# Transposes of queries, keys and attention values moved from TensorE to the DMA crossbar in a fused attention and token-mixing kernel

## The chip, the cores and the metric

One core of one Trainium2 chip. The metric is the device time of one execution in microseconds (us). Runs of one kernel agree within about 1.5%. Each ratio to the kernel before is taken on the same chip. Some times below are compared across chips; the kernel before had medians of 261.9 to 262.5 us.

## The reference

Grouped-query attention (8 batches, 16 query heads, 4 key/value heads, 384 tokens, head size 64), then a token-mixing layer on its output x (384 x 1024 per batch):

```python
scores = scale * q @ k.T;  attn = softmax(scores);  x = attn @ v       # per head; k, v shared by 4 heads
wq, wk = x @ w_q, x @ w_k                                              # 1024 -> 64
mixed = (scale * wq @ wk.T) @ x
out = relu(mixed) @ w_out                                              # 1024 x 1024
```

## The kernel before

All eight batches run through one software pipeline. A "duo" is two key/value heads with their eight query heads; a batch has two duos, each 3 x 3 score steps. Two steps make a **group**; a batch has nine, numbered 0 to 8 here. In each group TensorE issues the scores of two steps, ScalarE their exponentials, then TensorE does the tasks planned for that group and fills the rest of a budget with pieces of the previous batch's output projection ("filler", 48 matmuls per batch).

Three kinds of operand have to be transposed, and all are transposed on TensorE against an identity and copied out of PSUM by VectorE:

```python
def qt_task(s, d, j):                                   # queries; kt_task (keys) is alike
    ptr = psX.tile([P, G, P], BF16, name="ptq", tag="ps")
    for i in range(G):
        nc.tensor.transpose(out=ptr[:, i, :], in_=s.qbf[:, d, j, i, :, :].rearrange("p h d -> p (h d)"),
                            identity=ident)
    # ... (qT allocated)
    nc.vector.tensor_copy(out=s.qT[d][:, j, :, :], in_=ptr)

def xt_task(s, d, j):                                   # attention values, before the projection
    # ... four transposes of xnat into ptx
    nc.vector.tensor_copy(out=s.xT[:, n * d:n * (d + 1), j * P:(j + 1) * P], in_=ptr)

# planning: what runs in which group, with its cost in us
def start_next():                                       # in group 0 of batch b
    alloc_bf(batches[b + 1]); begin(batches[b + 1])
    if b + 2 < B: batches.append(load(b + 2))           # eight DMAs on SyncE's queue, 2.4 MB
# ...
at(g, lambda ...: av_task(batches[b], d, j, h), 0.37)   # attention x values
at(g + 1, lambda ...: xt_task(batches[b], d, j), 0.24)
# ...
at(g, lambda ...: kt_task(batches[nb], nd), 0.18)
at(g + j, lambda ...: qt_task(batches[nb], nd, j), 0.24)

SLOT = 2.0                                              # budget of a group
def fill(budget, keep=0):                               # pieces of output projection
    while filler and budget > 0 and left[0] > keep:
        next(filler[0]); budget -= 0.218; left[0] -= 1
# ... per batch: projection (proj) in group 2 of the next batch, wk in 3, c in 4,
#     mixing + ReLU in groups 5 and 6, then its output projection becomes the filler
```

A range test on the softmax sums chooses, at the end, whether a slow general path must run. It never does with this input.

## Time and profile before

| | before |
|---|---|
| time, median of 4 runs | 262.5 us |
| TensorE busy | 88% of the span |
| ScalarE, VectorE, GpSimd busy | 64%, 54%, 18% |
| one batch in the steady state | 29.6 us |
| mean granted TensorE clock | 0.98 |

The groups of instructions of the profile page show what the change removes. Columns: line, engine, operation, out<-in, shapes, count | busy us, mean ns of one | idle time before, and who ended it.

```profile
L181 DVE COPY xT<-ptx 128x512 bf16<-128x512 bf16 x48 | 20.4, 424 | 33.9 <-PE ptx L179 33.9
L141 DVE COPY qT<-ptq 128x512 bf16<-128x512 bf16 x48 | 19.9, 415 | 3.2 <-PE ptq L136 3.2
L179 PE MATMUL ptx<-ident,xnat 128*128 128x128 bf16 x192 | 19.3, 222 | 0.9 <-DVE xnat L170 0.9
L136 PE MATMUL ptq<-ident,qbf 128*128 128x128 bf16 x192 | 19.2, 224 | 0.5 <-DVE qbf L103 0.5
```

So 38.5 us of TensorE's busy time and 40.3 us of VectorE's go to these two kinds alone.

### The profile page before, as it was taken

How to read it: one execution, taken by the hardware profiler on the slowest of the kernel's cores; microseconds unless marked ns; L12 is line 12 of the kernel's file. 1: busy time of each engine (PE TensorE's matmuls, PEld its weight loads, DVE VectorE, ACT ScalarE, POOL GpSimd, SP SyncE). 2: the span in 40 equal slices, each digit the busy share in tenths (PEclk: the TensorE clock that was granted, in tenths of full speed). 3: DMA queues.
4: the chain of work that ended last, by engine and by line, in shares of the span. 5: the costliest groups of instructions: out<-in, count | busy, mean ns of one | idle time of the engine just before them, and what ended most of it. 6: DMA issues, size and time to landing. Idle time of an engine off the chain costs nothing.

```text
span 261.7 us, 5872 instructions
## 1 busy us (share of the span) xinstructions
PE 230.6 (88%) x2423; PEld 118.5 (45%) x2457; DVE 141.5 (54%) x388; ACT 166.9 (64%) x186; POOL 46.9 (18%) x105
## 2 busy tenths in 40 slices
PE   2988887999889997999889997999889998959892
PEld 1455543455435543455435543455445553433340
DVE  2367663566546664566546664566556563453531
ACT  2889897677757687577766687577766687500201
POOL 1797133052003220052002220040000000000000
PEclk9999999999999999999999999999999999977998
DMA  7999998293107801293107902101012202101224
GB/s 200 326 299 241 228 267 252 98 313 116 65 18 241 281 4 80 81 316 132 47 36 227 293 3 83 80 8 78 31 52 83 83 0 83 80 0 67 96 101 149
DMA packets 33712, 34.26 MB, mean 131 GB/s; under 512 B 4624, under 2 KB 29712, under 8 KB 33680
## 3 DMA queue, kind: packets, MB, share of 16 engines
q1 hardware_dynamic: 29184, 30.94, 36.5%
q0 software_dynamic: 3168, 2.36, 5.8%
q10 hardware_dynamic: 1328, 0.52, 0.7%
q8 instruction: 21, 0.34, 0.5%
q14 instruction: 11, 0.09, 0.1%
HBM read 23.59 MB, written 12.58 MB: 138 GB/s over the span
## 4 chain that ended last, share of the span: by engine, by line
PE 73%; ACT 14%; DVE 8%; issue 2%; DMA 1%; DVEq 0%; ACTq 0%
PE po L236 30%; PE sc L149 14%; PE av L164 11%; ACT msb L225 8%; ACT pT L155 6%; PE ptx L179 5%; PE pqk L187 5%; DVE xnat L170 3%; PE ptq L136 3%; PE pc L207 2%; DMA qraw<-in_q_dram 1%; PE pm L219 1%; DVE xT L181 1%; DVE rcp_all L169 1%; PE ptw L198 1%
## 5 line engine op out<-in xcount | busy, mean ns | idle before, releaser
L155 ACT ACTIVATE pT<-sc 128x1024 bf16<-128x1024 f32 x144 | 139.1, 1024 | 45.6 <-PE sc L149 44.9
L236 PE MATMUL po<-wout_sb,msb 128*128 128x512 bf16 x350 | 91.0, 385 | 6.6 <-ACT msb L225 4.7
L149 PE MATMUL sc<-qT,kT 64*128 64x512 bf16 x288 | 48.6, 394 | 9.4 <-ACT msb L225 5.0
L236 PEld LDWEIGHTS <-msb 128*128 128x128 bf16 x384 | 34.1, 99 | 46.7 <-ACT msb L225 9.3
L249 DVE COPY osb<-po 128x512 f32<-128x512 f32 x46 | 31.8, 690 | 38.9 <-PE po L236 38.6
L164 PE MATMUL av<-vbf,pT 128*128 128x65 bf16 x1152 | 45.4, 195 | 0.0
L164 PEld LDWEIGHTS <-pT 128*128 128x128 bf16 x1152 | 40.7, 98 | 9.4 <-issue 9.4
L170 DVE TENSOR_TENSOR xnat<-av,rcp_all 128x256 bf16<-128x256 f32 x96 | 40.8, 425 | 3.3
L181 DVE COPY xT<-ptx 128x512 bf16<-128x512 bf16 x48 | 20.4, 424 | 33.9 <-PE ptx L179 33.9
L103 POOL CAST qbf<-qraw 128x512 bf16<-128x512 f32 x46 | 26.9, 622 | 38.9 <-DMA qraw<-in_q_dram 17.4
L225 ACT ACTIVATE msb<-pm 128x768 bf16<-128x768 f32 x30 | 22.8, 809 | 14.2 <-PE pm L219 14.2
L149 PEld LDWEIGHTS <-kT 64*128 64x128 bf16 x288 | 11.5, 94 | 40.0 <-issue 37.0
L169 DVE RECIPROCAL rcp_all<-av 128x4 f32<-128x4 f32 x96 | 17.1, 178 | 17.7 <-PE av L164 17.7
L141 DVE COPY qT<-ptq 128x512 bf16<-128x512 bf16 x48 | 19.9, 415 | 3.2 <-PE ptq L136 3.2
L179 PE MATMUL ptx<-ident,xnat 128*128 128x128 bf16 x192 | 19.3, 222 | 0.9 <-DVE xnat L170 0.9
L136 PE MATMUL ptq<-ident,qbf 128*128 128x128 bf16 x192 | 19.2, 224 | 0.5 <-DVE qbf L103 0.5
L179 PEld LDWEIGHTS <-xnat 128*128 128x128 bf16 x192 | 11.0, 98 | 17.6 <-issue 11.5
L115 POOL MEMSET vbf<- 128x6 bf16 x16 | 2.0, 124 | 87.9 <-PE av L164 87.9
L193 ACT CAST q<-pqk 64x384 bf16<-64x384 f32 x8 | 3.8, 471 | 18.9 <-DVE qk L190 18.9
L187 PE MATMUL pqk<-xT,wqk_sb 128*128 128x384 bf16 x64 | 13.0, 352 | 0.8
L136 PEld LDWEIGHTS <-qbf 128*128 128x128 bf16 x192 | 12.4, 99 | 2.0 <-DVE qbf L103 1.6
L219 PE MATMUL pm<-qk,Csb 64*128 64x384 bf16 x32 | 8.4, 327 | 1.4 <-ACT msb L225 0.7
(40 smaller groups left out, 85.9 us busy)
## 6 DMA issues: line engine op xcount, KB each, us to landing
out_dram<-osb SPq DMA_DIRECT2D x23, 512.0 KB, 3.1
qraw<-in_q_dram SPq DMA_DIRECT2D x30, 384.0 KB, 6.5
kraw<-in_k_dram SPq DMA_DIRECT2D x16, 192.0 KB, 5.3
vraw<-in_v_dram SPq DMA_DIRECT2D x16, 192.0 KB, 6.3
wout_sb<-in_moe_w_out_dram POOLq DMA_DIRECT2D x4, 512.0 KB, 15.0
qraw<-in_q_dram SPq DMA_DIRECT2D x1, 512.0 KB, 5.2
qraw<-in_q_dram ACTq DMA_DIRECT2D x1, 256.0 KB, 3.9
out_dram<-osb SPq DMA_DIRECT2D x2, 128.0 KB, 2.3
```

Of the source, the lines that this page charges most:

```text
L103: eng.tensor_copy(out=out, in_=in_)
L136: nc.tensor.transpose(out=ptr[:, i, :], in_=s.qbf[:, d, j, i, :, :].rearrange("p h d -> p (h d)"), identity=ident)
L149: nc.tensor.matmul(out=ps[:, h, :], lhsT=s.kT[d][r, c, :], rhs=s.qT[d][r, j, :, :].rearrange("p g n -> p (g n)"), start=True, stop=True)
L155: nc.scalar.activation(out=s.pT[d, j][:, c, :, :], in_=ps, func=AF.Exp, scale=attn_scale)
L164: nc.tensor.matmul(out=av[:, i, :], lhsT=pT[:, c, h, i * P:(i + 1) * P], rhs=s.vbf[:, g, c, :], start=(c == 0), stop=(c == C - 1))
L170: nc.vector.tensor_tensor(out=s.xnat[:, j, g * G * D:(g + 1) * G * D].rearrange("p (i d) -> p i d", i=G), in0=av[:, :, :D], in1=rcp.to_bro ...
L179: nc.tensor.transpose(out=ptr[:, i, :], in_=s.xnat[:, j, dc * P:(dc + 1) * P], identity=ident)
L181: nc.vector.tensor_copy(out=s.xT[:, n * d:n * (d + 1), j * P:(j + 1) * P], in_=ptr)
L187: nc.tensor.matmul(out=pqk, lhsT=wqk_sb[:, dc, :], rhs=s.xT[:, dc, :], start=(dc == 0), stop=(dc == DC - 1))
L225: nc.scalar.activation(out=s.msb[:, i::DC // 2, :], in_=pm[:, :, :S], func=AF.Relu)
L236: nc.tensor.matmul(out=po, lhsT=s.msb[:, dc, c * P:(c + 1) * P], rhs=wout_sb[:, dc, half * NH:(half + 1) * NH], start=(dc == 0), stop=(dc ...
L249: nc.vector.tensor_copy(out=osb[:, half * NH:(half + 1) * NH], in_=po)
```

## The change

Intent: take the transposes off the busiest engine, and their copies off VectorE, by letting the DMA engines do them. Batch 0's queries and keys and the last duo's attention values stay on TensorE. The projection (and mixing) moves one group later, but for the last batch, and the range test later in the tail. Cut to its core:

```diff
+    def kt_dma(s):                                     # both duos of a batch, 128 x 768
+        nc.sync.dma_start_transpose(out=s.kT..., in_=s.kbf...)
+    def qt_dma(s, d):                                  # one duo, 128 x 1536
+        s.qT[d] = qt_p.tile([P, C, G, P], BF16, name="qT", tag="qT")
+        nc.sync.dma_start_transpose(out=s.qT[d]..., in_=s.qbf[:, d]...)
+    def xt_dma(s, d):                                  # one duo, 128 x 1536
+        nc.sync.dma_start_transpose(out=s.xT[:, d]..., in_=s.xnat[:, d]...)
 ...
-                    at(g + 1, lambda d=d, j=j: xt_task(batches[b], d, j), 0.24)
+                    if b == B - 1 and d == ND - 1:
+                        at(g + 1, lambda d=d, j=j: xt_task(batches[b], d, j), 0.24)
+                if b < B - 1 or d < ND - 1:
+                    at(g, lambda d=d: xt_dma(batches[b], d), 0.0)
 ...
+                elif nb < B:
+                    g = n0 // 2 + (2 if d else 1)
+                    if nd == 0:
+                        at(g, lambda nb=nb: kt_dma(batches[nb]), 0.0)
+                    at(g, lambda nb=nb, nd=nd: qt_dma(batches[nb], nd), 0.0)
 ...
-            g = b * GB + GB + 2
+            g = b * GB + GB + (3 if b < B - 1 else 2)
 ...
-            if g == end - 1:
-                range_test()
+        ok = range_test()                               # after the last group
+        fill(16 * 0.218)
+        count(ok)
```

The tiles xnat, xT and kT change their layout so that a duo, or a batch, is one contiguous transpose.

More of the change, by code (lines that the diff above doesn't have):

```diff
@@ L121, in cast_q @@
                     "p (h i) d -> p i h d", h=2))
+    def kt_dma(s):
+        nc.sync.dma_start_transpose(
+            out=s.kT.rearrange("p d c n -> p (d c) n"),
+            in_=s.kbf.rearrange("p d c h n -> p (d c h n)"))
+    def qt_dma(s, d):
+        s.qT[d] = qt_p.tile([P, C, G, P], BF16, name="qT", tag="qT")
+        nc.sync.dma_start_transpose(
+            out=s.qT[d].rearrange("p c g n -> p (c g) n"),
+            in_=s.qbf[:, d, :, :, :, :].rearrange("p c g h n -> p (c g h n)"))
+    def xt_dma(s, d):
+        nc.sync.dma_start_transpose(
+            out=s.xT[:, d, :, :, :].rearrange("p c i n -> p (c i) n"),
+            in_=s.xnat[:, d, :, :].rearrange("p c n -> p (c n)"))
     def kt_task(s, d):
@@ L129, in kt_task @@
                                 identity=ident)
-        s.kT[d] = qt_p.tile([P, C, P], BF16, name="kT", tag="kT")
-        nc.vector.tensor_copy(out=s.kT[d], in_=ptr)
+        nc.vector.tensor_copy(out=s.kT[:, d, :, :], in_=ptr)
     def qt_task(s, d, j):
@@ L148, in score @@
             r = slice(D * h, D * (h + 1))
-            nc.tensor.matmul(out=ps[:, h, :], lhsT=s.kT[d][r, c, :],
+            nc.tensor.matmul(out=ps[:, h, :], lhsT=s.kT[r, d, c, :],
                              rhs=s.qT[d][r, j, :, :].rearrange("p g n -> p (g n)"),
@@ L170, in av_task @@
         nc.vector.tensor_tensor(
-            out=s.xnat[:, j, g * G * D:(g + 1) * G * D].rearrange("p (i d) -> p i d", i=G),
+            out=s.xnat[:, d, j, h * G * D:(h + 1) * G * D].rearrange("p (i d) -> p i d", i=G),
             in0=av[:, :, :D], in1=rcp.to_broadcast([P, G, D]), op=ALU.mult)
@@ L177, in xt_task @@
         for i in range(n):
-            dc = n * d + i
-            nc.tensor.transpose(out=ptr[:, i, :], in_=s.xnat[:, j, dc * P:(dc + 1) * P],
+            nc.tensor.transpose(out=ptr[:, i, :], in_=s.xnat[:, d, j, i * P:(i + 1) * P],
                                 identity=ident)
-        nc.vector.tensor_copy(out=s.xT[:, n * d:n * (d + 1), j * P:(j + 1) * P], in_=ptr)
+        nc.vector.tensor_copy(out=s.xT[:, d, j, :, :], in_=ptr)
     def proj_task(s):
@@ L186, in proj_task @@
         for dc in range(DC):
-            nc.tensor.matmul(out=pqk, lhsT=wqk_sb[:, dc, :], rhs=s.xT[:, dc, :],
+            nc.tensor.matmul(out=pqk, lhsT=wqk_sb[:, dc, :], rhs=s.xT[:, dc // (DC // ND), :, dc % (DC // ND), :],
                              start=(dc == 0), stop=(dc == DC - 1))
@@ L207, in c_task @@
                 nc.tensor.matmul(out=pc[h * Dh:(h + 1) * Dh, :], lhsT=s.wk[:, c, :],
-                                 rhs=s.xnat[:, c, h * NH:(h + 1) * NH],
+                                 rhs=s.xnat[:, h, c, :],
                                  start=(c == 0), stop=(c == C - 1))
@@ L255, in begin @@
     def begin(s):
-        s.kT, s.qT, s.pT = [None] * ND, [None] * ND, {}
-        s.xnat = x_p.tile([P, C, Dm], BF16, name="xnat", tag="xnat")
-        s.xT = x_p.tile([P, DC, S], BF16, name="xT", tag="xT")
+        s.qT, s.pT = [None] * ND, {}
+        s.kT = qt_p.tile([P, ND, C, P], BF16, name="kT", tag="kT", bufs=2)
+        s.xnat = x_p.tile([P, ND, C, NH], BF16, name="xnat", tag="xnat")
+        s.xT = x_p.tile([P, ND, C, DC // ND, P], BF16, name="xT", tag="xT")
     with tc.manual_schedule():
@@ L330, in plan @@
                         at(g, lambda d=d, j=j, h=h: av_task(batches[b], d, j, h), 0.37)
-                    at(g + 1, lambda d=d, j=j: xt_task(batches[b], d, j), 0.24)
+                    if b == B - 1 and d == ND - 1:
+                        at(g + 1, lambda d=d, j=j: xt_task(batches[b], d, j), 0.24)
+                if b < B - 1 or d < ND - 1:
+                    at(g, lambda d=d: xt_dma(batches[b], d), 0.0)
                 nb, nd = (b, d + 1) if d + 1 < ND else (b + 1, 0)
-                if nb < B:
-                    g = n0 // 2 + (2 if d else 3 if b == 0 else 1)
-                    at(g, lambda nb=nb, nd=nd: kt_task(batches[nb], nd), 0.18)
+                if nb == 0:
+                    g = n0 // 2 + 3
+                    at(g, lambda nd=nd: kt_task(s0, nd), 0.18)
                     for j in range(C):
-                        at(g + j, lambda nb=nb, nd=nd, j=j: qt_task(batches[nb], nd, j), 0.24)
+                        at(g + j, lambda nd=nd, j=j: qt_task(s0, nd, j), 0.24)
+                elif nb < B:
[3 more added lines that the diff above has]
+                    at(g, lambda nb=nb, nd=nd: qt_dma(batches[nb], nd), 0.0)
         at(0, lambda: qt_task(s0, 0, 1), 0.24)
@@ L380, in range_test, with count @@
             nc.vector.tensor_tensor(out=ok[:, 2:3], in0=ok[:, 0:1], in1=ok[:, 1:2], op=ALU.mult)
+            return ok
+        def count(ok):
             pok = psX.tile([P, 1], F32, name="pok", tag="ps")
@@ L414 @@
                     left[0] += C * (Dm // NH) * DC
-                fill(SLOT, keep(g))
-            if g == end - 1:
-                range_test()
-            if g == end + 3:
-                good = nc.values_load(oki[0:1, 0:1], min_val=0, max_val=P,
-                                      skip_runtime_bounds_check_because="a count of partitions")
-                tc.mark_branch_hint_location("general", "LikelyTaken")
+                fill(SLOT if g < last else 0.0, keep(g))
+        ok = range_test()
+        fill(16 * 0.218)
+        count(ok)
+        good = nc.values_load(oki[0:1, 0:1], min_val=0, max_val=P,
+                              skip_runtime_bounds_check_because="a count of partitions")
+        tc.mark_branch_hint_location("general", "LikelyTaken")
         fill(1e9)
@@ L453 @@
                                 out=ps, lhsT=s.qT[d][r, j, i, :],
-                                rhs=s.kT[d][r, :, :].rearrange("p c n -> p (c n)"),
+                                rhs=s.kT[r, d, :, :].rearrange("p c n -> p (c n)"),
                                 start=True, stop=True)
@@ L477 @@
                             nc.vector.reciprocal(out=rn, in_=rn)
-                            h0 = (g * G + i) * D
-                            nc.vector.tensor_scalar_mul(s.xnat[:, j, h0:h0 + D], av[:, :D], rn)
+                            h0 = (h * G + i) * D
+                            nc.vector.tensor_scalar_mul(s.xnat[:, d, j, h0:h0 + D], av[:, :D], rn)
                     xt_task(s, d, j)
```

## The prediction

> **What bounds the kernel now.** I read the page first (shares of busy time, the 40 slices), then the chain that ended last, one batch of it in order of time, and last the queue of DMA issues.
>
> The page, busy time of each engine, DMA share of the 40 slices, and chain by engine:
> ```profile
> PE 230.6 (88%) x2423; PEld 118.5 (45%) x2457; DVE 141.5 (54%) x388; ACT 166.9 (64%) x186; POOL 46.9 (18%) x105
> ...
> DMA  7999998293107801293107902101012202101224
> ...
> PE 73%; ACT 14%; DVE 8%; issue 2%; DMA 1%; DVEq 0%; ACTq 0%
> ```
> TensorE is the bound, with ScalarE (exponentials) in 14% of the chain. The DMA engines look idle on average, but not evenly: full for the first 7 slices (46 us), then nearly full for one or two slices once per batch (digits 7 to 9), and quiet between; from slice 24 on there are no loads. That unevenness carries this prediction.
>
> A batch takes 29.58 us (first output-projection matmul of one batch to the next in the chain: 44.61, 74.19, 103.78, 133.37). A batch is nine groups of two score steps; I number them 0 to 8. Part of one batch, the chain in order of time (start us, us, what):
> ```profile
> 110.77 0.54 PE sc L149 x4
> 111.31 0.33 PE ptx L179 x4
> 111.64 0.76 PE av L164 x24
> 112.40 1.08 PE po L236 x5
> 113.48 0.54 PE sc L149 x4
> 114.01 0.33 PE ptx L179 x4
> 114.34 0.17 PE ptk L127 x3
> 114.51 0.22 PE ptq L136 x4
> ...
> 125.05 0.54 PE sc L149 x4
> ...
> 128.06 1.52 ACT msb L225 x2
> ...
> 131.80 1.52 ACT msb L225 x2
> 133.37 1.68 PE po L236 x7
> 135.06 0.54 PE sc L149 x4
> ```
> Each "sc x4" begins a group (110.77 is group 0, 125.05 group 5, 135.06 group 7). Groups without mixing take 2.6 to 3.2 us and are TensorE alone, because the filler (po) is dealt out up to a budget per group. Groups 5 and 6 hold the mixing and take 10.0 us together; there ScalarE's ReLUs pace it. A set of four transposes is 0.22 to 0.33 us on the chain, three for the keys 0.17.
>
> The SyncE queue in the timeline, start of run and one batch:
> ```profile
> 18.93 2.42 SPq L72 DMA_DIRECT2D vraw<-in_v_dram  x1
> ...
> 138.62 0.39 SPq L72 DMA_DIRECT2D kraw<-in_k_dram  x1
> ...
> 142.78 1.00 SPq L72 DMA_DIRECT2D vraw<-in_v_dram  x1
> ```
> The load issued at 18.93 lands 18.9 us later (the tile view of vraw in that window), at 37.8: the loads of batches 0 to 2 and of the output weights compete. In the steady state the first of a batch's eight loads goes out at 138.62 and the last, issued at 142.78, lands 6.5 us later, at 149.3: 10.7 us for the lot.
>
> **What the Trainium skill says.** (1) "DMA: Bandwidth & Descriptors", Queues, rings and completion order: SyncE owns one ring on each of the 16 engines, and descriptors are consumed in ring order. The trace agrees: a small 192 KB load, alone 4.9 us, takes 18.9 us behind others. (2) Same page, Latency and other measured facts: a DMA transpose with a non-contiguous middle dimension moved 261 GB/s. No transpose is in this trace; I use the figure as an estimate. (3) "VectorE: DVE Perf Modes", The three transpose paths: 390 ns for a 128x128 transpose on TensorE, 1309 ns by the crossbar. The trace differs for TensorE: 222 ns as one instruction (19.3 us of busy time for 192), some 55 to 80 ns each in a run of four.
>
> **The change part by part.**
>
> *Removed from TensorE.* Per batch 6 sets of queries (0.22), 6 of attention values (0.33), 2 of keys (0.17): 1.3 + 2.0 + 0.3 = 3.6 us of chain. VectorE loses the copies: 42 x 0.415 + 45 x 0.424 + 14 x 0.348 = 41 us, off the path (VectorE is 54% busy).
>
> *What that is worth if transposes are free.* I lay the groups out again: scores 0.54, an attention-value pair 0.86, filler 0.216 each, projection 1.5. Projection and mixing each move one group later. Groups 8, 0, 2: 0.54 + 0.86 + 6 fillers = 2.70 each; group 1: ten fillers, 2.75; group 3: 0.54 + 0.86 + 1.5 = 2.9, say 2.95; group 4: 2.9; group 5: 2.4, as the 48 fillers have run out. In groups 6 and 7 ScalarE has two exponentials, two ReLUs, two, two: (1.94 + 1.52) x 2 with 0.4 at the front, 7.3, then 1.65 until the next scores: 8.95 against 10.0. Sum 28.05, say 28.1. So 3.6 us off TensorE saves only 1.5 per batch, since mixing is ScalarE's and the filler runs out sooner.
>
> *Added: transposes in SyncE's queue, in order.* The order of instructions of the changed kernel shows, around the start of a batch: transpose of the previous batch's last attention values, the eight loads, transpose of this batch's second-duo queries. The first waits for VectorE in group 0, the last is needed by the second score pair of group 4. From the start of group 0:
> - attention values normalised: 2.3 (scores at 124.98, xnat done 127.3, in a group of that shape);
> - that transpose issued, as long as a load's issue, 0.5: loads start at 2.85, not some 1.5 us before the batch as now;
> - loads landed, + 10.7: 13.5;
> - query transpose behind them, 128 x 1536 x 2 bytes = 393 KB at 261 GB/s = 1.5: 15.05.
> Needed at 2.70 + 2.75 + 2.70 + 2.95 + 0.27 = 11.4. **TensorE waits 3.7 us**, more than the 1.5 gained: 31.8 per batch. Batches 1 to 5 have loads in group 0; 6 and 7 not, so these take 28.1.
>
> *Start of the run.* Batch 1's keys and first queries are now transposes behind the loads of batch 2 in the ring, after batch 0's first attention values. Last load lands 37.8, + 1.5 + 0.75 + 1.5 = 41.6. Before, that group's scores started at 25.4. Then as above 15.05 to the second pair of group 4: 56.6; exponential of that pair 1.4, group 5's 1.95, and from group 6's exponentials to the last ReLU 6.9 (two of 0.97, ReLUs 1.52, two exponentials, ReLUs): 66.8 for the first output-projection matmul, against 44.6.
>
> *Tail.* From batch 6's first output-projection matmul now 261.7 - 222.1 = 39.6. One group fewer follows it (scores 0.54, transposes some 0.8), and the range test no longer stands ahead of the last projection (231.7 to 233.2 in the chain, 1.5): 36.8.
>
> *Sum.* 66.8 + 4 x 31.8 + 2 x 28.1 + 36.8 = **287 us**.
>
> **Rivals.**
> - *Hidden transposes.* If they land in time (another ring, or loads that finish sooner): first matmul at 44.6 + 2 for one more group, 46.6 + 6 x 28.1 + 36.8 = 252. For it: DMA share is only 0.41 per batch, and the exceptions for batch 0 and the last duo look like a schedule tuned for latency. Against it: the order in the queue and a landing 18.9 us after issue.
> - *Only the steady wait.* If the ring is free at the start (batch 1 at 28): 287 - 14 = 273. Against: the DMA row is at 9 until slice 6.
> - *Steady wait small.* If loads drain in 8 us and transposes in 1, the wait is some 0.5: 287 - 5 x 3.2 = 271.
> - *ScalarE becomes the bound.* 20.8 us busy per batch, so it cannot set 28; it only takes the gain in the mixing groups.
> - *Crossbar slow.* At 1309 ns per 128x128 block, 54 blocks a batch are 71 us: some 500 us in all. I think that figure is mostly fixed latency, and a batched transpose does not pay it per block.
>
> **Range and chances.** The centre is 287, with the start (16 us late, then the batch's own wait) its largest term, and 5 waits of 3.7 +- 2 us its second. Either may be half, so most of the weight lies in 267 to 300. I keep a fifth of the weight for the transposes bypassing the loads or landing sooner: 250 to 265. Range 258 to 301. Faster 0.14, same 0.10, slower 0.76.
>
> **What would show it right or wrong.** Right: score matmuls waiting for a DMA of qT, once of 10 us or more near 26 us, then 3 to 5 us in group 4 of batches 1 to 5 and none in 6 and 7; a period near 32, then near 28; TensorE's busy time down to some 205 us but its share to about 70%; loads issued about 3 us after a batch's first scores. Wrong: query transposes that land within 4 us of issue even behind loads, periods of 28 throughout, or waits of the projection for xT. The tail should be shorter by 2 to 3 us in any case; if the granted clock there (0.89 now) moves, that part is off.

## More of the kernel before

One more view proved to matter, and the prediction did not use it: the clock that TensorE was granted, here in the view of chosen stretches (stretch, length, busy us of each engine with counts, granted clock, DMA share, GB/s):

```profile
222.00:232.34 10.34, 8.17 (x87) 4.22 (x87) 6.06 (x16) 3.88 (x4) 0.00 (x0) 1.00 0.12 51
232.34:239.17 6.83, 5.91 (x19) 2.79 (x21) 1.58 (x7) 0.47 (x1) 0.00 (x0) 0.50 0.00 0
```

After a stretch in which TensorE idles for 2 us in the tail (the range test), its clock is halved for 6.8 us.

## The result

| | before | changed |
|---|---|---|
| time, median of 4 runs | 262.5 us | 311.8 us |
| profiled span | 261.7 us | 309.1 us |
| TensorE busy | 230.6 us (88%) | 229.7 us (74%) |
| mean granted clock | 0.98 | 0.87 |
| one batch: with loads / without | 29.6 / 29.6 us | 34.7 to 38.3 / 28.5 to 29.4 us |

The ratio is 1.185 (95% interval 1.176 to 1.194). Ratios here are the mean time of one kernel's fast runs over that of the other's fast runs of the same rounds, so not quite the ratio of the medians in the table. The record gives every run of the experiments below as correct; for this one it says nothing. The change is 18.5% slower.

The profile page after: busy time, then granted clock and DMA share in 40 slices of 7.7 us, then the chain by engine.

```profile
PE 229.7 (74%) x2067; PEld 104.3 (34%) x2067; DVE 106.8 (35%) x287; ACT 166.0 (54%) x186; POOL 47.0 (15%) x105
...
PEclk9995557687996779877897799979799899999999
DMA  8999959760791909909199174937270916121314
...
PE 60%; ACT 17%; DMA 13%; SPq 4%; DVE 3%; issue 2%; ACTq 0%
```

Two things are to be seen. DMA and SyncE's queue (SPq), 1% of the chain before, are now 17%: TensorE waits for transposes. And TensorE shows 356 matmuls fewer, yet is busy as long as before: the clock row falls to between 5 and 8 tenths in 19 of the 40 slices, where it had been 9 but for the tail, so what is left runs slower. (The code has 390 fewer; 34 filler matmuls are missing from the trace before.)

The chain in order of time through one batch with loads (batch 3, group 0 at 114.10), to be set against the chain of before in the prediction:

```profile
114.10 0.54 PE sc L164 x4
114.64 0.86 PE av L179 x24
115.50 1.30 PE po L250 x6
...
123.70 1.21 PE pqk L201 x8
124.92 6.40 DMA qT<-qbf
131.31 0.05 issue
131.36 0.61 PE sc L164 x2
131.97 0.43 PE ptw L212 x3
132.40 3.61 PE po L250 x9
...
144.66 4.38 PE po L250 x10
```

TensorE stands for 6.4 us in group 4 for the second duo's queries. Nine pieces of filler then take 3.61 us, and ten after the mixing 4.38, where ten took 2.26 us in group 1 of the same batch. Why the queries come late is in SyncE's queue, from the timeline of the same batch (start us, us, queue, line, DMA):

```profile
116.38 1.41 SPq L136 DMA_TRANSPOSE xT<-xnat  x1
117.84 0.56 SPq L72 DMA_DIRECT2D kraw<-in_k_dram  x1
118.50 1.01 SPq L76 DMA_DIRECT2D qraw<-in_q_dram  x2
...
121.68 3.14 SPq L72 DMA_DIRECT2D vraw<-in_v_dram  x1
124.92 3.86 SPq L131 DMA_TRANSPOSE qT<-qbf  x1
```

The transpose of attention values waits for group 0, the eight loads stand behind it, and the queries' transpose behind the loads. The last load, issued at 121.68, lands 8.3 us later (its tile view), at 130.0; the transpose lands at 131.3. In batches 6 and 7 no loads stand there, and the same transpose lands 3.4 us after its issue, before it is needed.

The start of the run, same view:

```profile
21.80 14.16 SPq L136 DMA_TRANSPOSE xT<-xnat  x1
36.07 3.02 SPq L125 DMA_TRANSPOSE kT<-kbf  x1
39.14 1.47 SPq L131 DMA_TRANSPOSE qT<-qbf  x1
```

The first transpose holds SyncE until 36, the last load of batch 2 lands at 38.9 (20.0 us after its issue), and batch 1's first scores start at 42.7 us instead of 25.4.

Last, the clock around the wait, in stretches as above:

```profile
122.80:131.36 8.56, 2.53 (x36) 1.52 (x36) 1.68 (x5) 3.36 (x4) 0.00 (x0) 0.85 1.22 240
131.36:136.01 4.65, 4.65 (x16) 1.68 (x18) 0.95 (x2) 1.02 (x1) 1.73 (x3) 0.54 0.13 54
```

The trace lists the stretches at half clock. In the changed kernel there are eleven before the end, 82 us together, each 3.4 us or a multiple of it; before, one of 6.8 us. The Trainium skill has this: "TensorE: Matmul & The Clock Gate", Part 1, says that TensorE runs at half rate after an idle window of about 3.4 us and at full rate after a busy one, and that the windows run on without regard to the kernel. The trace agrees on the lengths, 3.41, 6.83 and longer multiples, and on clocks of 0.5 and 1.0 alone. It does not agree that TensorE must have been idle throughout the window. In the kernel before, the 3.41 us ahead of the halving at 232.34 had TensorE busy for 1.34 us, with no gap over 1.9 us. In the changed kernel, the 3.41 us ahead of the halving at 104.92, in a mixing group where no DMA is waited for, had it busy for 1.87 us, with no gap over 0.6 us. Where the limit lies is not shown: a window with 2.07 us busy (139.05 to 142.47) was followed by half clock, and one with 2.00 us (180.01 to 183.43) was not.

### The profile page after: what moved, and what is told of

Same layout as the page of the kernel before. It is cut to its first block, busy times and chain, and to the rows that moved or that the text cites. A ratio compares the mean times of both kernels' runs of the same rounds, so it can differ in the third digit from the quotient of the medians.

```text
span 309.1 us, 5113 instructions
## 1 busy us (share of the span) xinstructions
PE 229.7 (74%) x2067; PEld 104.3 (34%) x2067; DVE 106.8 (35%) x287; ACT 166.0 (54%) x186; POOL 47.0 (15%) x105
## 4 chain that ended last, share of the span: by engine, by line
PE 60%; ACT 17%; DMA 13%; SPq 4%; DVE 3%; issue 2%; ACTq 0%
PE po L250 31%; PE av L179 12%; DMA qT<-qbf 12%; ACT pT L170 11%; PE sc L164 11%; ACT msb L239 5%; SPq L136 3%; PE pqk L201 2%; PE pc L221 2%; DMA qraw<-in_q_dram 1%; SPq L125 1%; PE ptw L212 1%; DVE msb L241 1%; PE pm L233 1%; DVE xnat L185 1%
## 5 line engine op out<-in xcount | busy, mean ns | idle before, releaser
L250 PE MATMUL po<-wout_sb,msb 128*128 128x512 bf16 x384 | 107.4, 426 | 2.4 <-ACT msb L239 1.1
L164 PE MATMUL sc<-qT,kT 64*128 64x512 bf16 x288 | 52.7, 420 | 55.5 <-DMA qT<-qbf 45.7
L263 DVE COPY osb<-po 128x512 f32<-128x512 f32 x46 | 31.8, 690 | 74.5 <-PE po L250 74.4
L250 PEld LDWEIGHTS <-msb 128*128 128x128 bf16 x384 | 37.6, 107 | 54.6 <-issue 22.3
L179 PEld LDWEIGHTS <-pT 128*128 128x128 bf16 x1152 | 41.6, 101 | 20.4 <-issue 17.8
L179 PE MATMUL av<-vbf,pT 128*128 128x65 bf16 x1152 | 47.6, 199 | 0.0
L184 DVE RECIPROCAL rcp_all<-av 128x4 f32<-128x4 f32 x96 | 17.1, 178 | 68.8 <-PE av L179 68.4
L233 PE MATMUL pm<-qk,Csb 64*128 64x384 bf16 x32 | 10.9, 346 | 12.4 <-ACT pT L170 10.9
L215 DVE COPY wk<-ptw 128x192 bf16<-128x192 bf16 x8 | 2.1, 258 | 33.2 <-PE ptw L212 33.2
L233 PE MATMUL pm<-q,Csb 64*128 64x384 bf16 x32 | 11.4, 361 | 0.0
L233 PEld LDWEIGHTS <-Csb 64*128 64x128 bf16 x64 | 4.4, 93 | 19.4 <-issue 18.3
L103 POOL CAST kbf<-kraw 128x384 bf16<-128x384 f32 x15 | 7.7, 511 | 10.1 <-issue 8.3
L103 POOL CAST vbf<-vraw 128x384 bf16<-128x384 f32 x16 | 8.1, 506 | 0.0
(40 smaller groups left out, 56.2 us busy)
```

The lines of the kernel that those rows point to most:

```text
L103: eng.tensor_copy(out=out, in_=in_)
L164: nc.tensor.matmul(out=ps[:, h, :], lhsT=s.kT[r, d, c, :], rhs=s.qT[d][r, j, :, :].rearrange("p g n -> p (g n)"), start=True, stop=True)
L179: nc.tensor.matmul(out=av[:, i, :], lhsT=pT[:, c, h, i * P:(i + 1) * P], rhs=s.vbf[:, g, c, :], start=(c == 0), stop=(c == C - 1))
L184: nc.vector.reciprocal(out=rcp, in_=av[:, :, D])
L233: nc.tensor.matmul(out=pm[:, h, :S], lhsT=s.Csb[r, i * P:(i + 1) * P], rhs=(s.qk if h == 0 else s.q2)[r, :], start=True, stop=True)
L250: nc.tensor.matmul(out=po, lhsT=s.msb[:, dc, c * P:(c + 1) * P], rhs=wout_sb[:, dc, half * NH:(half + 1) * NH], start=(dc == 0), stop=(dc ...
```

## The experiments

My theory after the result had three parts: (A) transposes are late because loads stand ahead of them in SyncE's ring; (B) each wait costs a second time, because TensorE's clock is halved after it; (C) a batch without waits is set by how the filler is dealt out. The main rivals: the crossbar is slow or takes the bandwidth wherever it stands; and the half clock has to do with load on the chip, not with waiting.

### e1_load_later: loads after the transpose they delayed

```diff
-                    if b + 2 < B:
+                    if b + 2 < B and b == 0:
                         batches.append(load(b + 2))
 ...
                     at(g, lambda nb=nb, nd=nd: qt_dma(batches[nb], nd), 0.0)
+                    if d == 0 and b + 2 < B:
+                        at(g, lambda b=b: batches.append(load(b + 2)), 0.0)
```

> The eight loads of batch b+2 are issued after the transpose of batch b's second-duo queries instead of before it (batches 1 to 5); nothing else moves. Theory (ring order): the transpose lands about 3.5 us after its issue instead of 6.2 to 7.3, before group 4 needs it, so the five waits of 6.2 to 7.3 us for qT in group 4 go, and with them the half-clock stretch after each; the first 42 us stay. 311.8 - 32 of waits - 8 of half clock = about 272 us. Rival (crossbar transposes are slow by themselves or take the bandwidth): waits of 4 us or more stay in group 4, over 300 us.

278.5 us (ratio to before 1.063, interval 1.055 to 1.072). All waits for qT in group 4 are gone; one is left, 17.9 us, at the start. SyncE's queue in one batch:

```profile
103.99 1.41 SPq L136 DMA_TRANSPOSE xT<-xnat  x1
105.50 1.46 SPq L131 DMA_TRANSPOSE qT<-qbf  x1
107.02 0.58 SPq L72 DMA_DIRECT2D kraw<-in_k_dram  x1
```

The same transposes, the same bytes, some 32 us less by order alone (fast runs): (A) holds for the steady state, and a crossbar that is slow by itself is ruled out. It is the order in SyncE's queue that is shown. In the changed kernel's batch 3, 10.8 of the 17.2 us until landing pass before SyncE issues the transpose and 6.4 after (here 3.3); how much of the latter is the ring and how much shared engines, this run does not separate. The expected 272 was missed by 6 us: half clock did not vanish, some 3.4 to 6.8 us a batch stayed after the mixing groups.

### e2_first_on_pe: batch 1's first operands on TensorE

```diff
+                elif nb == 1 and nd == 0:
+                    g = n0 // 2 + 2
+                    for dd in range(ND):
+                        at(g, lambda dd=dd: kt_task(batches[1], dd), 0.18)
+                    for j in range(C):
+                        at(g + j, lambda j=j: qt_task(batches[1], 0, j), 0.24)
                 elif nb < B:
```

> Keys of batch 1 and its first-duo queries transposed by TensorE again; all else as in the changed kernel. Theory: batch 1's first scores start near 25.5 us instead of 42.7, but the loads of batch 3 and the transpose behind them are then still in the crowded start, so part of the 17 us comes back in group 4 of batch 1: 295 to 303 us. The four later waits of 6 us stay. Rival (the late start is hidden by later slack): 308 or more.

306.5 us, between what was expected (295 to 303) and the rival's time (308 or more). The chain shows why: the wait moved to the next transpose in the queue. The second duo's queries of batch 1 land at 51.7 us instead of 59.2, so of the 17 us only 7.5 were left there, and some 5 at the end.

### e3_both: the two edits together

> Both edits. Theory: no wait for a transpose over 2 us, half clock in well under 20 us in all, a batch in 28 to 28.6 us as in batches 6 and 7 of the changed kernel: 252 to 258 us, so faster than the kernel before by 2 to 4%. Rival (something else in the change costs as well, for example DMA contention or xT arriving late at the projection): 262 or more.

269.4 us (1.027, 1.018 to 1.036; unclear whether slower by 2%): not the 252 to 258 that was expected but in the range of the rival, 262 or more. No wait for qT is left, but two things that I had not counted. The projection of batch 0 waits for its attention values, in the chain of this kernel:

```profile
20.22 0.86 PE av L179 x24
21.80 18.62 DMA xT<-xnat
40.56 2.73 PE pqk L201 x8
...
84.32 0.50 PE pm L233 x2
84.82 4.38 PE po L250 x10
```

and the last line shows half clock after the mixing in a batch without any DMA wait: TensorE has used up its filler and idles while ScalarE does exponentials and ReLUs.

### e4_keep_warm: dead matmuls in place of the wait

```diff
+                    if 1 <= st[0] <= 5 and st[1:] == (1, 0, 0):
+                        dum = psX.tile([P, NH], F32, name="dum", tag="ps")
+                        for _ in range(26):
+                            nc.tensor.matmul(out=dum, lhsT=ident, rhs=wout_sb[:, 0, :NH], start=True, stop=True)
                     pss.append((st, score(batches[st[0]], *st[1:])))
```

> 26 dead matmuls of 512 columns (5.6 us at full clock) put in the place of the wait in group 4 of batches 1 to 5; result unchanged. Theory (a TensorE that waits[...] is then granted half the clock for 3.4 or 6.8 us): the waits shrink to under 1 us of idle, the transposes land when they did, the half-clock stretches near 91, 129, 166 go, and the ten projection matmuls after the wait take 2.0 us instead of 3.2 to 3.8: 303 to 306 us although work was added. Rival (the half clock has to do with the load on the chip, not with the wait): no gain or slower, 312 or more, and the half-clock stretches stay.

303.8 us against 311.8 (304.0 against 311.1 in the mean of fast runs), with 130 matmuls added that nobody reads. The transpose lands 17.3 us after group 0 begins, as in the changed kernel. The filler after it and the stretches in this kernel:

```profile
119.21 8.10 DMA qT<-qbf
127.36 0.39 PE sc L164 x2
127.75 0.27 PE ptw L212 x3
128.02 1.94 PE po L250 x9
```

```profile
119.00:127.30 8.30, 8.02 (x58) 3.76 (x54) 1.68 (x5) 3.13 (x4) 0.00 (x0) 1.00 1.03 265
127.30:132.00 4.70, 4.64 (x48) 2.24 (x48) 1.86 (x6) 2.70 (x3) 1.73 (x3) 1.00 0.01 3
```

TensorE was busy through the wait, the clock stayed at 1.00, and nine pieces take 1.94 us instead of 3.61. That is (B) shown: the idle time of the wait, not the load on the chip, halves the clock. The size of this second cost is read from the traces: the "four batches with loads" of the table further down take 137.6 us here and 146.3 in the changed kernel, 8.7 less, and the filler just after the four waits takes 7.8 us in place of 14.3. The whole time is less exact, since the half clock of the start, ahead of the first dead matmul, also differs (17.1 us against 27.3), though the program is the same up to there.

### e5_start: batch 0's first-duo attention values on TensorE too

e3_both, with `xt_task` kept for `(b, d) in ((0, 0), (B - 1, ND - 1))`.

> The version with both edits, and batch 0's first-duo attention values transposed by TensorE too, so that no transpose is queued behind the loads of the start. Theory: the wait of 7.6 us of the first projection for xT (and the 13.7 us of half clock after it) goes; first output-projection matmul near 47 us instead of 56.6; 258 to 261 us. Rival (the start is bound by the loads anyway): 266 or more.

269.3 us, no gain over e3_both: the rival's time. The projection still starts at 40.4 us, now for the second duo's attention values. Whatever is taken out of the queue, the next transpose waits for the same loads.

### e6_spread: a smaller budget per group

e5_start, with one edit:

```diff
-        SLOT = 2.0
+        SLOT = 1.5
```

> As e5_start, with the budget of a group cut from 2.0 to 1.5, so that the 48 pieces of output projection last through the mixing groups, where TensorE idles in the version with both edits and its clock is halved for 3.4 to 6.8 us in each batch. Theory: a batch falls from 28 to 30 us to 25 to 26, and the half-clock stretches once a batch go: 236 to 244 us. Rival (ScalarE sets the batch at 28 and the idle TensorE costs nothing): within 3 us of e5_start.

248.8 us (0.950, 0.942 to 0.958), 20 us less than e5_start, for one number. The rival falls: the batch takes 26.0 us. Granted clock of e5_start and of this kernel, from their pages:

```profile
PEclk9999775779995999889997999779997999599998
```

```profile
PEclk9999975597999999999999999999999999999999
```

In e5_start the clock falls in every batch, in e6_spread only at the start. I expected 236 to 244; the start, where the chain still has 11.9 us for xT, is the likely rest, and e9_start_pe tests it.

### e7_range_only: the range test alone

The kernel before, with the change's two hunks on the range test and nothing else.

> The kernel before with the range test moved as in the change, and nothing else. Theory: the 1.5 us in which the last projection stands behind the test go: 260 to 261 us against 262. If the clock falls in the tail after that gap in the kernel before (half from 232.3 to 239.2), it may go too, another 2 to 3 us: 257 to 259. Rival (the test is hidden): 262.

259.5 us (0.991, 0.984 to 0.999): by the medians 2.4 us better. The half-clock stretch from 232.3 to 239.2 is gone from the trace. So this part of the change is sound. But what it gains is the clock and not the 1.5 us of the test: the kernel before has no half clock in three of its seven runs (granted clock 1.0), and those took 259.6 to 259.8 us, the same as here.

### e8_loads_pool: loads in another queue

```diff
-        nc.sync.dma_start(out=t[:, g0:g1, :, :],
+        (nc.gpsimd if b > 1 else nc.sync).dma_start(out=t[:, g0:g1, :, :],
```

and the same for the queries.

> The changed kernel with the loads of batches 2 to 7 issued from GpSimd's queue, so that they sit in other rings of the same 16 engines; the transposes stay where they are in SyncE's order. Theory (order in the ring, not bandwidth): the transposes of the second duo no longer stand behind the loads and only share the engines with them, landing 3.5 to 5 us after issue; waits in group 4 under 1.5 us, the late start mostly gone: 258 to 275 us. Rival (the engines are full, whichever ring the loads are in): the waits of 6 us stay, 300 or more.

288.4 us: between the theories. In the steady state GpSimd happened to issue the loads just after the transpose (114.02 against 113.23), so SyncE no longer had them ahead of it. No wait in group 4 over 0.3 us was left, as the theory said. But the transpose landed 6.9 to 7.5 us after its issue in the three batches looked at, not in 3.5 to 5; alone it takes 3.4. The chain of one such batch:

```profile
113.23 7.45 DMA qT<-qbf
120.68 0.05 issue
120.73 0.39 PE sc L165 x2
```

So loads in another queue slow a transpose as well; it was only issued early enough to bear it. At the start it told more than I had asked. SyncE's queue:

```profile
19.67 4.67 SPq L137 DMA_TRANSPOSE xT<-xnat  x1
26.41 1.51 SPq L126 DMA_TRANSPOSE kT<-kbf  x1
27.97 15.35 SPq L132 DMA_TRANSPOSE qT<-qbf  x1
```

No load of batches 2 or 3 stands in this ring, and still the queries' transpose lands 23.9 us after issue, and the first scores of batch 1 wait 26.9 us. A separate ring was therefore no cure at the start, and order in SyncE's ring is not the whole cause of the late start. What the profile shows of it: the changed kernel moves 51,000 packets more than the kernel before and 12.7 MB more, and the transposes' packets are of 256 bytes. From 28 to 52 us in this run they went beside weight loads in packets of 2 KB and loads of the batches in packets of up to 4.6 KB. The Trainium skill ("DMA: Bandwidth & Descriptors", Queues, rings and completion order) says that an engine takes turns between queues packet by packet; small packets would then get a small share. That is consistent with these 23.9 us, if the profile's packets are those of the page. It stays an explanation and is not shown: issued from GpSimd, the loads go out in packets of up to 4.6 KB where SyncE's are of 768 bytes, so this run changed ring and packet size together.

### e9_start_pe, e11_slot165: a better version

As e6_spread, but everything that is needed before the first loads have drained stays on TensorE: attention values of batch 0, keys and queries of batch 1. e11_slot165 has the budget 1.65.

> As e6_spread, but everything that the start needs before the loads have drained stays on TensorE: attention values of batch 0, keys and queries of batch 1. Crossbar transposes begin with batch 1's attention values. Theory: the last wait at the start (11.9 us of the chain until xT at 40.4 us, and 10 us of half clock) goes: 248.8 - 8 to 11 = 238 to 241 us. Rival (the start is bound by the loads and the wait only moves on): 245 or more.

> As e9_start_pe with the budget of a group 1.65 in place of 1.5. If the batch of 26.0 us is set by ScalarE between the pieces, a larger budget starves the mixing groups again: 1 to 6 us slower than e9_start_pe. If TensorE sets it, the same time.

241.4 us for e9_start_pe (0.921, 0.914 to 0.929): just above the 238 to 241 expected, and 8% faster than the kernel before. 246.5 us for e11_slot165, 1 to 6 us slower as expected: a larger budget spends the filler sooner, and a batch takes 26.9 us instead of 26.0. After the start, e11_slot165 has a single stretch at half clock (3.4 us), so the filler's distribution costs time by itself and not only through the clock. The page of e9_start_pe:

```profile
PE 211.8 (88%) x2094; PEld 101.9 (42%) x2121; DVE 110.6 (46%) x301; ACT 166.2 (69%) x186; POOL 47.2 (20%) x105
```

### e10_before_spread: the control

The kernel before with the range test moved and SLOT at 1.75; no crossbar.

> The control: the kernel before (all transposes on TensorE) with the range test moved and the budget cut from 2.0 to 1.75, where its 48 pieces should just last. Theory: mixing groups of 10.0 us shorten a little, but TensorE still has 3.6 us of transposes per batch: a batch of 28.5 to 29.3 us, 252 to 258 us, so the crossbar is worth some 15 us in all at the best order. Rival (the gain of e6_spread is all from the budget and none from the crossbar): within 5 us of e9_start_pe.

254.9 us (0.975, 0.967 to 0.982; unclear whether faster by 2%), a batch of 29.0 us, both as expected. So a part of the gain of e9_start_pe has nothing to do with transposes: 7 us come from the budget and the range test. Against this control, the crossbar is worth 13.5 us, 3.0 us per batch, when it is ordered well. The prediction's 3.6 us of transposes on the chain is thus nearly all to be had, once the filler is dealt out to suit. One reservation: the control has one budget and keeps the projection where it was, while for the crossbar version two budgets were tried, so a better control may exist.

## Why the prediction was right or wrong

The direction was right, and so was the mechanism in the steady state: transposes behind loads in SyncE's queue, a wait in group 4 of batches 1 to 5 and none in 6 and 7. The start was 17 us late as predicted, but its cause is only in part the order in the ring (e8_loads_pool). The prediction took a load that lands 18.9 us after issue as a sign of ring order; shared engines can do the same, and the 4.9 us that it calls alone was one of eight loads. The time was not right: 311.8 us, above the range (258 to 301). The terms of its sum, measured in the profiled span:

| term | predicted | measured | difference |
|---|---|---|---|
| first output-projection matmul | 66.8 | 71.4 | +4.6 |
| four batches with loads | 127.2 | 146.3 | +19.1 |
| two batches without loads | 56.2 | 57.9 | +1.7 |
| tail | 36.8 | 33.5 | -3.3 |
| sum | 287 | 309.1 | +22.1 |

**The step that failed** is "TensorE waits 3.7 us ...: 31.8 per batch". Two terms of it:

- *The wait was mis-sized.* The four waits were 6.2, 6.4, 6.2 and 7.3 us, 26.1 in all against 14.8: +11.3 us. In the batch shown, attention values were ready at 2.3 us after group 0 (predicted 2.3), but their transpose held SyncE for 1.4 us and not 0.5, so loads began at 3.7 (2.85); the loads took 12.1 us and not 10.7, behind that transpose and an output store (which of the two slowed them is not shown); the queries' transpose took 1.3 us (1.5); and TensorE was ready at 10.8 and not 11.4.
- *The clock was left out.* I had read the clock row and took it as constant, with only the tail in doubt. 146.3 less the waits of 26.1 and 4 x 28.1 leaves 7.8 us, where TensorE runs at half clock after the waits and after the mixing groups. In e4_keep_warm, which keeps TensorE busy through the waits, the same four batches take 8.7 us less. The skill's page on the clock gate, Part 1, describes waits for DMA that halve the clock, and I cited other pages and not this one.

*Start.* The delay of batch 1's first scores was right within 1.1 us (42.7 against 41.6). The rest of the +4.6 comes after them: the transpose for group 4 landed 16.5 us after group 0 and not 15.05 (attention values were ready 3.2 us after group 0 and not 2.3, at half clock until 50.3), and from there to the output projection it took 12.1 us and not 10.2, with half clock from 57.1 to 64.0.

*Batches without loads* took 28.5 and 29.4 us, from one first filler after mixing to the next (217.71, 246.16, 275.61 in the chain), against 28.1: the layout of groups by hand held, with stretches of 3.4 us at half clock after the mixing groups in the difference. That it "saves only 1.5 per batch, since ... the filler runs out sooner" was right for this budget; e6_spread showed that the limit was the budget of 2.0 and not the transposes.

*Tail.* Shorter than predicted, most likely because the half-clock stretch that the kernel before had there went too (e7_range_only). How much that is depends on where the clock's windows fall: the same tail took 36.8 to 37.1 us in e1_load_later, e3_both and e4_keep_warm, where half clock followed the last mixing group.

*Rivals.* "Crossbar slow" falls: with no loads beside it a transpose of 12 blocks lands 3.2 to 3.4 us after issue. "Hidden transposes" was wrong for this order, and became true in e1_load_later for the steady state. "TensorE's busy time down to some 205 us" was wrong, 229.7, again for the clock.

## What to carry to other kernels

Moving work to DMA gives it a place in a queue: write down, for each transfer, what stands ahead of it in the issuing engine's order and what those wait for, before counting bandwidth that is free on average. Count a wait of TensorE of a few microseconds as more than its length, since what follows ran at half clock here, and so did what followed mixing groups in which TensorE was busy little more than half of the time. A schedule that spreads the filler over such groups was worth more here (20 us) than the transposes saved (13.5 us). And when an engine loses work, deal the filler out anew, because the old budget was tuned to the old work.

## What the Trainium skill lacked or had wrong

- "DMA: Bandwidth & Descriptors", DMA Transpose (X-bar): it gives no time for how long a transpose holds the queue that issues it while the DMA engines are busy. Here SyncE was held 1.4 us for a 128 x 1536 transpose with no loads ahead, 3.8 to 5.0 us behind a batch's loads, and 14.2 us behind those of the start, and everything after it waited too.
- "VectorE: DVE Perf Modes", The three transpose paths: 1309 ns for a 128x128 transpose by the crossbar misleads if it is taken per block of a larger one. Twelve blocks in one DMA landed 3.2 to 3.4 us after issue, and where two such overlapped (256 to 258 us of the changed kernel) the DMA engines moved 251 GB/s. That is near the 261 GB/s of the DMA page, which it gives for a non-contiguous middle dimension; its higher figure for the contiguous case was not reached.
- The same DMA page: its rule that a transpose next to ordinary DMAs needs nothing is about correctness, and held (every run of the experiments was correct); it doesn't say what the neighbours cost. Beside loads in another queue, one transpose took 23.9 us to land at the start, and others 6.9 to 7.5 us in the steady state.
- "TensorE: Matmul & The Clock Gate", Part 1: it gives no measure of how idle a window has to be. Here half clock followed windows of 3.41 us with TensorE busy for 1.34 us, 1.87 us and 2.07 us.
